# A fused attention and feed-forward kernel: first chunk in two token halves, first groups of 2, 2, 4 and 8 slices, all steps reordered

## The chip, the cores and the metric

The kernel runs on one core of a Trainium2 chip. The metric is the time on the device of that core, in microseconds (us). Most executions of one kernel lie within 1% of each other. An execution that is more than 1.5% above the fastest of its kernel is called slow.

## The reference

A sketched attention (four batches, four heads, 1088 tokens, 32 columns a head) is followed by a feed-forward with a rational activation:

```python
def phi(x):                                   # 8 x 8 features a token and head
    a = np.einsum('rd,bhsd->bhsr', S1, x)
    b = np.einsum('rd,bhsd->bhsr', S2, x)
    return np.einsum('bhsi,bhsj->bhsij', a, b).reshape(*x.shape[:-1], r * r)

q_p, k_p = phi(q), phi(k)
kv  = np.einsum('bhsf,bhsd->bhfd', k_p, v)    # one small matrix a batch and head
z   = np.sum(k_p, axis=2)
x   = np.einsum('bhsf,bhfd->bhsd', q_p, kv) / (np.einsum('bhsf,bhf->bhs', q_p, z)[..., None] + 1e-06)
# x becomes 4352 tokens x 128
h = x @ w_in                                  # 128 -> 2048
P = a[0] + a[1] * h + a[2] * h**2 + a[3] * h**3
Q = 1.0 + abs(b[0]) * abs(h) + abs(b[1]) * h**2
out = (P / (Q + 1e-06)) @ w_out               # 2048 -> 128
```

## The kernel before

The tokens run in chunks of 512 (the last is 256). The 2048 hidden columns are 16 slices of 128, and a group is a few slices of one chunk that share their operations. The program is a list of steps, each with an engine, the steps it needs and the buffers it takes and gives. Three tables written ahead of time decide the rest: `ORDER` (the sequence in which the steps are issued; it fixes each engine's queue), `ENGINE` (ScalarE or VectorE for a step that either can do) and `HOME` (which PSUM buffer a small result uses).

```python
FIRST = [4, 4, 8]      # slices in the groups of the first chunk
LAST = [8, 4, 4]       # slices in the groups of the last, short chunk; all others: 8, 8
# ... ENGINE, HOME, ORDER = [27, 4, 26, 30, ...]  (589 steps)

def issue(self, order):
    # ... each step in turn: its needs must be done, its buffers free
    for i in order:
        s = self.steps[i]
        s["fn"]()
```

A chunk's x is made in one piece: numerator and denominator (PE), division (VectorE), transposes (PE), copy to `xT` with a sign (either engine). Step names: `q0.nd0`, `q0.nd1`, `q0.dv`, `q0.xt`, `q0.xe`.

```python
def divide():
    nb = min(2, nt)
    nd = pair("nd")[:, :nt // nb, :nb * 132].rearrange("p b (g c) -> p b g c", c=D + 1)
    den = new("den", n)[:, :nt // nb, :nb * H]
    nc.vector.tensor_scalar(out=den, in0=nd[:, :, :, D], scalar1=1e-6, scalar2=None, op0=AX.add)
    nc.vector.reciprocal(out=den, in_=den)
    # ... x = nd * den
def x_transposes():
    p = new(*ps(nm, "xT"))
    for i in range(nt):
        nc.tensor.transpose(p[:, i * 128:(i + 1) * 128], in_=T["x", n][:, i, :], identity=ident)
```

A group g then goes through these steps; the letters are the step names used below:

```python
# h0, h2, ..: hidden matmuls, two slices each (PE), into h_ps
# e0, e2, ..: cast to bf16 hb (ScalarE, sometimes VectorE)
# ab: u = |hb|     sq: s = hb*hb      hi: t = a3*hb + a2
# cu: t = t*s      lo: hb = a1*hb+a0  (all VectorE)
def add(dst, src, name):                      # us: u += s  and  ts: t += hb
    d, s = T[dst, g][:, :gw], T[src, g][:, :gw]
    if ENGINE.get(name) == "DVE":
        nc.vector.tensor_add(out=d, in0=d, in1=s)
    else:
        nc.gpsimd.dma_start(out=d, in_=s, accum_op=AX.add, max_dma_last_dim=4096)
# ln: L = log(lsc*u + 1), ex: u = exp(-L)     (ScalarE)
# ov: t = t*u (VectorE)   pj: projection (PE)
```

So the first sum `us` and the second sum `ts` of nearly every group are accumulating transfers, and ScalarE's logarithm waits for the first.

## Time and profile before

| | before |
|---|---|
| median of 3 runs | 251.03 us (249.64 to 251.61) |
| span of the profiled execution | 248.8 us |
| accumulating transfers (first queue; 0.52 MB of it loads `w_out`) | 34.87 MB, 79.7% of the 16 engines' time |

The table by stretch is the view on which the explanation rests. Columns: stretch, length, then busy time and number of instructions of PE, PE's weight loads, VectorE (DVE), ScalarE (ACT) and GpSimd (POOL), then the granted clock, the DMA share and GB/s. The prediction shows its row for 20 to 30 us; these are further rows of the kernel before:

```profile
30.00:40.00 10.00, 9.86 (x59) 4.94 (x58) 9.90 (x12) 8.92 (x8) 1.72 (x2) 1.00 1.18 166
40.00:120.00 80.00, 78.38 (x682) 44.35 (x680) 74.98 (x59) 73.35 (x60) 15.67 (x12) 1.00 0.96 185
120.00:140.00 20.00, 19.99 (x186) 11.14 (x184) 19.90 (x15) 19.90 (x15) 3.57 (x3) 1.00 0.96 177
205.00:252.00 47.00, 24.86 (x215) 18.81 (x213) 37.73 (x35) 37.15 (x21) 8.36 (x8) 0.85 0.83 156
```

To read it: length less busy time is what an engine idled. VectorE idles 0.10 us between 120 and 140 us and 5.02 us between 40 and 120.

### The profile page before, as it was taken

How to read it: one execution, taken by the hardware profiler on the slowest of the kernel's cores; microseconds unless marked ns; L12 is line 12 of the kernel's file. 1: busy time of each engine (PE TensorE's matmuls, PEld its weight loads, DVE VectorE, ACT ScalarE, POOL GpSimd, SP SyncE). 2: the span in 40 equal slices, each digit the busy share in tenths (PEclk: the TensorE clock that was granted, in tenths of full speed). 3: DMA queues.
4: the chain of work that ended last, by engine and by line, in shares of the span. 5: the costliest groups of instructions: out<-in, count | busy, mean ns of one | idle time of the engine just before them, and what ended most of it. 6: DMA issues, size and time to landing. Idle time of an engine off the chain costs nothing.

```text
span 248.8 us, 4279 instructions
## 1 busy us (share of the span) xinstructions
PE 222.5 (89%) x1789; PEld 127.1 (51%) x1789; DVE 225.4 (91%) x205; ACT 213.7 (86%) x158; POOL 48.8 (20%) x61
## 2 busy tenths in 40 slices
PE   7999999999999999998999899999998969920763
PEld 2674455654636465553657354546453627720532
DVE  0785999998989989998999999999999999998993
ACT  3335589989989798989999999899999899899990
POOL 4000422132101212121111221122031312113210
PEclk9999999999999999999999999999999999995599
DMA  5994498999998899979999999999999999999982
GB/s 149 315 278 172 72 147 173 174 219 185 176 169 182 147 192 223 232 166 173 169 177 202 171 171 171 211 169 171 189 172 186 182 201 187 179 184 186 200 162 68
DMA packets 23427, 45.11 MB, mean 181 GB/s; under 512 B 5232, under 2 KB 13552, under 8 KB 23408
## 3 DMA queue, kind: packets, MB, share of 16 engines
q0 software_dynamic: 11232, 34.87, 79.7%
q1 hardware_dynamic: 11712, 9.90, 12.6%
q8 instruction: 14, 0.23, 0.4%
q10 hardware_dynamic: 464, 0.08, 0.2%
q14 instruction: 5, 0.04, 0.0%
HBM read 8.79 MB, written 2.23 MB: 44 GB/s over the span
## 4 chain that ended last, share of the span: by engine, by line
DVE 31%; PE 31%; DMA 20%; ACT 10%; issue 8%; SPq 0%; DVEq 0%; ACTq 0%; POOLq 0%
PE h_ps L572 15%; DMA u<-s 12%; DVE t L621 7%; DVE s L582 6%; DMA t<-hb 5%; DVE t L607 4%; DVE u L585 4%; PE h_ps L499 4%; ACT u L618 4%; DVE t L603 3%; PE out_ps L629 3%; ACT L L614 3%; DVE hb L610 2%; ACT hb L184 2%; DMA q<-in_q_dram 2%
## 5 line engine op out<-in xcount | busy, mean ns | idle before, releaser
L572 PE MATMUL h_ps<-xT,w_in_sb 128*128 128x512 f32 (+1 forms) x288 | 126.0, 577 | 4.2 <-ACT hb L184 2.7
L572 PEld LDWEIGHTS h_ps<-xT,w_in_sb 128*128 128x128 f32 x288 | 51.7, 190 | 56.5 <-issue 43.1
L184 ACT CAST hb<-h_ps 128x1024 bf16<-128x1024 f32 x66 | 64.8, 1020 | 8.2 <-PE h_ps L572 7.8
L614 ACT ACTIVATE L<-u,one_ap,lsc 128x4096 f32<-128x4096 bf16 (+2 forms) x20 | 65.9, 3295 | 6.4 <-DMA u<-s 6.3
L618 ACT ACTIVATE u<-L 128x4096 bf16<-128x4096 f32 (+2 forms) x20 | 62.3, 3116 | 0.2
L629 PE MATMUL out_ps<-w_out,t 128*128 128x128 bf16 x544 | 35.2, 225 | 15.8 <-DVE t L621 15.7
L594 POOL DMA_DIRECT2D u<-s x19 | 24.1, 1269 | 118.9 <-DVE u L585 54.5
L629 PEld LDWEIGHTS <-t 128*128 128x128 bf16 x544 | 32.5, 101 | 23.8 <-DVE t L621 20.6
L621 DVE TENSOR_TENSOR t<-t,u 128x4096 bf16<-128x4096 bf16 (+2 forms) x20 | 39.2, 1968 | 4.0 <-ACT u L618 2.2
L582 DVE TENSOR_TENSOR s<-hb 128x4096 bf16<-128x4096 bf16 (+2 forms) x20 | 39.2, 1963 | 1.5 <-ACT hb L184 1.5
L607 DVE TENSOR_TENSOR t<-t,s 128x4096 bf16<-128x4096 bf16 (+2 forms) x20 | 39.3, 1967 | 0.3
L594 POOL DMA_DIRECT2D t<-hb x18 | 21.6, 1200 | 72.2 <-issue 20.1
L610 DVE TENSOR_SCALAR hb<-hb,a_sb 128x4096 bf16<-128x4096 bf16 (+2 forms) x20 | 23.8, 1189 | 0.2
L603 DVE TENSOR_SCALAR t<-hb,a_sb 128x4096 bf16<-128x4096 bf16 (+2 forms) x20 | 23.6, 1183 | 0.0
L585 DVE TENSOR_SCALAR u<-hb 128x4096 int16<-128x4096 int16 (+2 forms) x20 | 22.3, 1115 | 0.1
L499 PE MATMUL h_ps<-qT,Srep 64*128 64x512 f32 (+1 forms) x72 | 19.5, 617 | 0.4 <-ACT hb L184 0.4
L506 DVE TENSOR_TENSOR q_pT<-A_sb,h_ps 128x1024 f32<-128x1024 f32 (+1 forms) x9 | 10.4, 1157 | 2.6 <-ACT A_sb L184 1.4
L519 PEld LDWEIGHTS h_ps<-kv,q_pT 128*64 128x64 f32 (+1 forms) x288 | 8.7, 134 | 5.1 <-issue 2.0
L519 PE MATMUL h_ps<-kv,q_pT 128*64 128x66 f32 (+1 forms) x288 | 10.1, 224 | 0.0
L184 ACT COPY A_sb<-h_ps 128x1024 f32<-128x1024 f32 (+1 forms) x9 | 8.7, 965 | 0.8 <-PE h_ps L499 0.8
L499 PEld LDWEIGHTS h_ps<-qT,Srep 64*128 64x128 f32 x72 | 5.4, 184 | 6.9 <-ACT hb L184 2.1
L184 ACT COPY kT<-h_ps 128x512 f32<-128x512 f32 x5 | 2.9, 585 | 5.3 <-PE h_ps L383 4.8
(89 smaller groups left out, 137.0 us busy)
## 6 DMA issues: line engine op xcount, KB each, us to landing
u<-s POOLq DMA_DIRECT2D x15, 1024.0 KB, 8.6
t<-hb POOLq DMA_DIRECT2D x15, 1024.0 KB, 9.5
k_sb<-in_k_dram SPq DMA_DIRECT2D x4, 512.0 KB, 4.3
q<-in_q_dram SPq DMA_DIRECT2D x8, 256.0 KB, 4.9
v<-in_v_dram SPq DMA_DIRECT2D x4, 512.0 KB, 8.2
out_dram<-oT SPq DMA_DIRECT2D x8, 256.0 KB, 7.0
w_in_sb<-in_moe_w_in_dram SPq DMA_DIRECT2D x2, 512.0 KB, 4.8
u<-s POOLq DMA_DIRECT2D x2, 512.0 KB, 7.7
```

The source lines that it names most:

```text
L184: nc.scalar.copy(out=out, in_=in_)
L499: nc.tensor.matmul(pair(i)[:, g, :W], lhsT=Srep[i][rows].rearrange("p g f -> p (g f)"), rhs=T["qT", n][rows, :W], start=True, stop=True)
L572: nc.tensor.matmul(p[:, i * W:(i + 1) * W], lhsT=w_in_sb[:, fi * 128:(fi + 1) * 128], rhs=T["xT", n][:, :W], start=True, stop=True)
L582: nc.vector.tensor_mul(out=new("s", g)[:, :gw], in0=h, in1=h)
L585: nc.vector.tensor_scalar(out=new("u", g)[:, :gw].bitcast(mybir.dt.int16), in0=T["hb", g][:, :gw].bitcast(mybir.dt.int16), scalar1=0x7FFF, ...
L594: nc.gpsimd.dma_start(out=d, in_=s, accum_op=AX.add, max_dma_last_dim=4096)
L603: nc.vector.tensor_scalar(out=new("t", g)[:, :gw], in0=T["hb", g][:, :gw], scalar1=a_sb[:, 3:4], scalar2=a_sb[:, 2:3], op0=AX.mult, op1=AX ...
L607: nc.vector.tensor_mul(out=T["t", g][:, :gw], in0=T["t", g][:, :gw], in1=T["s", g][:, :gw])
L614: nc.scalar.activation(out=new("L", g, l0)[:, :lw], in_=T["u", g][:, l0:l0 + lw], func=ACT.Ln, bias=one_ap, scale=lsc)
L618: nc.scalar.activation(out=T["u", g][:, l0:l0 + lw], in_=T["L", g, l0][:, :lw], func=ACT.Exp, scale=-1.0)
L621: nc.vector.tensor_mul(out=T["t", g][:, :gw], in0=T["t", g][:, :gw], in1=T["u", g][:, :gw])
L629: nc.tensor.matmul(T["out_ps", n][:, j * 128:(j + 1) * 128], lhsT=T["t", g][:, c:c + 128], rhs=W_out[:, fis[i], :], start=fis[i] == 0 and ...
```

## The change

Its intent: VectorE and ScalarE idle in the first 25 us, so the first chunk's x is made in two halves of 256 tokens, and its first feed-forward groups are small, so that VectorE starts on them earlier. Then every step was ordered anew, with other choices of engine and buffer. The core of the diff (the three tables are cut, and so is an unused variant that goes):

```diff
-FIRST = [4, 4, 8]
+FIRST = [2, 2, 4, 8]
+SPLIT = [0]
 # ENGINE, HOME and ORDER: all replaced (ORDER now has 604 steps)
-        def divide():
+        def divide(part=None):
             nb = min(2, nt)
-            nd = pair("nd")[:, :nt // nb, ...]
+            b0, b1 = (0, nt // nb) if part is None else (part, part + 1)
+            nd = pair("nd")[:, b0:b1, ...]
             ...
-        def x_transposes():
+        def x_transposes(part=None):        # the transposes of one half
-        def x_evac():
+        def x_evac(part=None):              # the copy of one half to xT
+        if n in SPLIT:
+            out = []
+            for i in range(2):
+                s = plan.add(f"{nm}.dv{i}", "DVE", 830, lambda i=i: divide(i), after=[nd[i]] + out[-1:], ...)
+                s = plan.add(f"{nm}.xt{i}", "PE", 240, lambda i=i: x_transposes(i), after=[s], ...)
+                out.append(add_copy(f"{nm}.xe{i}", lambda i=i: x_evac(i), W // 2, ...))
+            return out
...
+            if n in SPLIT and fis[s] == 0:   # first pair of slices: one half of the tokens at a time
+                hm = plan.add(f"{nm}.i{s}", "PE", 880, lambda s=s: h_mm(s, 0), ...)
+                hm = plan.add(f"{nm}.h{s}", "PE", 880, lambda s=s: h_mm(s, 1), ...)
```

## The prediction

> **What bounds the kernel now.** I read the page's busy shares first, then the forty slices, then the table by stretch, then the gaps of VectorE in order of time, and the chain of waits last.
>
> ```profile
> PE 222.5 (89%) x1789; PEld 127.1 (51%) x1789; DVE 225.4 (91%) x205; ACT 213.7 (86%) x158; POOL 48.8 (20%) x61
> ...
> DVE  0785999998989989998999999999999999998993
> ACT  3335589989989798989999999899999899899990
> ...
> DMA  5994498999998899979999999999999999999982
> ```
>
> The averages name VectorE (91%), with PE, ScalarE and the DMA engines close behind. The slices (6.2 us each) show where the missing 9% lies: VectorE is at 0, 7, 8 and 5 tenths in the first four and near full from 25 us on. In slices 4 and 5 (19 to 31 us) the DMA engines are at 4 tenths and ScalarE at 5.
>
> ```profile
> 20.00:30.00 10.00, 10.00 (x27) 4.69 (x28) 8.37 (x13) 5.04 (x7) 2.56 (x2) 1.00 0.29 79
> 40.00:60.00 20.00, 19.51 (x201) 11.37 (x200) 18.64 (x16) 18.26 (x17) 4.95 (x4) 1.00 0.96 185
> 140.00:160.00 20.00, 19.15 (x143) 10.29 (x142) 19.82 (x17) 18.98 (x12) 3.78 (x3) 1.00 1.01 186
> 220.00:235.00 15.00, 3.41 (x33) 3.41 (x34) 13.72 (x13) 14.90 (x7) 3.83 (x4) 0.59 1.04 189
> ```
>
> The columns are stretch, length, busy time of PE, PEld, DVE, ACT and POOL, granted clock, DMA share and GB/s. From 40 us on nothing is free: of 20 us, VectorE works 18.6 to 19.8, ScalarE 18.3 to 19.0, and the DMA share is 0.96 to 1.01. Only 20 to 30 us has room: there PE computes the first hidden slices and the others wait for them. In 220 to 235 PE is nearly done, while ScalarE and DMA are full.
>
> ```profile
> 16.73 0.69 DVE L529 TENSOR_TENSOR x<-h_ps,den 128x512 f32<-128x512 f32 x1
> 17.34 1.21 DVE L403 TENSOR_TENSOR k_p<-a_t,w_ps 128x1024 f32<-128x1024 f32 x1
> 19.95 1.22 DVE L506 TENSOR_TENSOR q_pT<-A_sb,h_ps 128x1024 f32<-128x1024 f32 x1 [1.41 <-ACT A_sb L184]
> ...
> 24.68 1.23 DVE L582 TENSOR_TENSOR s<-hb 128x2048 bf16<-128x2048 bf16 x1 [1.46 <-ACT hb L184]
> ```
>
> VectorE divides the first chunk's x at 16.2 to 17.4 us, but squares its first hidden group only at 24.68, after gaps of 1.41 and 1.46 us. Between them lie four transposes, the copy of x to xT (18.33, 0.69 us), the first hidden matmuls (from 19.90) and two casts (21.92 and 23.63), since a group of 4 slices needs two casts. This stretch is what the change attacks. Later gaps are small and have several owners:
>
> ```profile
> 59.88 2.29 DVE L621 TENSOR_TENSOR t<-t,u 128x4096 bf16<-128x4096 bf16 x1 [0.74 <-ACT u L618]
> 71.22 1.22 DVE L506 TENSOR_TENSOR q_pT<-A_sb,h_ps 128x1024 f32<-128x1024 f32 x1 [0.67 <-PE h_ps L499]
> ...
> 90.59 0.29 DVE L186 COPY a_t<-w_ps 128x128 f32<-128x128 f32 x1 [0.99 <-PE w_ps L392]
> ```
>
> The seven larger ones between 41 and 116 us are 0.49, 0.74, 0.67, 0.40, 0.99, 0.68 and 0.65: 4.6 us in all. From 120 to 222 us VectorE is busy 100.57 of 102.
>
> ```profile
> DVE 31%; PE 31%; DMA 20%; ACT 10%; issue 8%; SPq 0%; DVEq 0%; ACTq 0%; POOLq 0%
> ```
>
> The chain of waits moves from engine to engine: no single wait can be removed for its full length.
>
> **What the Trainium skill says.** "Perfetto Trace Analysis", section "Optimizing Scalar/DVE Operations": if these engines are not saturated but cause bubbles on others, "breaking up instructions may allow work to be completed sooner". That is the idea here, and the trace agrees that both have room before 25 us and not after. "VectorE: DVE Perf Modes", section "The TRN2 errata": a large tile pays a fixed cost once, many small tiles pay it each. The trace agrees: the bf16 product takes 2288, 1215 and 686 ns for 4096, 2048 and 1024 columns, so 0.524 ns a column and some 140 ns fixed. "DMA: Bandwidth & Descriptors", section "Issuing engines are not separate DMA queues": all transfers share 16 engines and interleave. The trace agrees: an accumulate of 256 KB landed in 3.7 us at the quiet end, and two others of that size took 7.4 in the median.
>
> **The change part by part.** I decoded both orders into the sequence of steps on each engine; the number of fill matmuls stays (15 of 16 run), and no arithmetic changes. The unused path with four weight copies goes: no instruction of it ran.
>
> *The start.* Up to the key-value products of the first batch (PE until 13.6) the queues are nearly the same. Then, with durations of the trace: the two kv copies end at 14.6 (one on each engine, as before); the first half's numerator matmuls take 0.55 (half of 1.09), to 15.4; an expansion of the second chunk (1.06) follows, then the other half's 0.55, to 17.0. The first half's division (0.16+0.20+0.43, as in the last chunk's rows of half the width) runs beside them, to 16.3. Its two transposes end at 17.3, its copy to xT, now on VectorE (0.48), at 17.9; the second division at 18.7. PE meanwhile does a key projection (0.6) and the second expansion (1.06), so the second transposes end at 19.2 and their copy at 19.7. The first half's hidden matmuls stand in PE's queue behind those transposes, so the two halves gain little by themselves: 19.2 to 20.1 for both slices. The cast of a group of two slices is one (20.2 to 21.2, before: the second ended at 24.64). VectorE, which first does the small constants (1.05) and a key product (1.13), begins the first group at 22.0 in place of 24.68. Its gaps in this stretch are then some 0.5 and 0.6 us in place of 1.41 and 1.46, with work enough after 22 because slices 4 to 7 arrive next and slices 2 and 3 are left for later: **1.7 us saved**.
>
> *What VectorE pays.* Two divisions for one: 2 x (159+203+425) - (170+253+691) = +0.46 us. The copy to xT moves from ScalarE: 2 x 477 ns = +0.95. One more group (2048 columns become two of 1024): six operations more; by their starts (1.13 becomes 2 x 0.60 for a product, 0.72 becomes 2 x 0.46 for a scalar operation) about +0.67. The other moves between the engines nearly cancel: 9.95 us leave VectorE (one 2048-column sum of each kind at 1.22, one of 1024 at 0.69, two casts, three output copies, four smaller) and 9.22 come (three sums of 1024 columns, three casts, two output copies, six smaller): -0.73. Sum: **+1.35 us**.
>
> *ScalarE*: -0.69 for the copy, +0.4 for one more pair of logarithm and exponential (2 x 1242 - 2097 and 2 x 1057 - 1913, less overlap), -0.3 for the rest: **-0.6 us**, no relief worth counting.
>
> *DMA.* The sums done by accumulate were 67,584 + 66,560 columns and become 68,608 + 67,584, because VectorE takes three small ones in place of two of 2048 and one of 1024: +1.5%. Their queue took 79.7% of 248.8 us, so 198 us: **+3.0 us** of transfer. Against it the first sum is issued at about 23.3 in place of 26.83, and the engines were idle from 22 to 28.
>
> *Sum.* On VectorE -1.7 + 1.35 = -0.35 us. The larger hope is the middle: the first sums land some 3 us earlier, so logarithms fill ScalarE while PE still makes hidden slices, and PE finishes seven of the first chunk's eight pairs of slices about 1.5 us earlier. I assume that two fifths of the 4.6 us of gaps go, 1.85 us; this is a choice, not a reading. That makes -2.2 us: 251.0 - 2.2 = **248.8 us**.
>
> **Rivals.** *The gain is eaten.* ScalarE sets the pace to the end: from 217.76 it runs to 243.1 almost without a gap. From its first cast at 21.92 it idles 15.7 us; it starts 1.5 us earlier in the change, but 1.9 us of small work done before that point has moved away or later. If its later gaps stay, nothing is won: 251. Its waits for first sums speak for this rival (6.3 us in eight waits, second only to those for hidden matmuls, 7.8), since the DMA work grows. *DMA becomes the bound.* With 3.0 us more transfer and a start 3.5 us earlier, a full DMA would end at the same time: 250.5 to 252. Against: VectorE waited only 1.8 us for the second sums in the whole run. *The new order dissolves the middle gaps.* All 4.6 us gone with -0.35 gives 246.1; for it speaks that each such gap is under 1 us and that an order can be searched for; against it that PE, ScalarE and DMA are over 95% busy there. *A worse tail.* The last groups need the same ScalarE work in the same order of sizes, about 25 us, and the last product and store cost the same; I count nothing either way.
>
> **Range and chances.** From full failure with one new wait (251.8) to nearly all gaps gone (245.8): that should hold 8 times in 10. Faster by over 2% needs 246.0 or less, thus every gap: 0.12. Slower by over 2% would need 5 us of new waits: 0.04. Within 2%: 0.84.
>
> **What would show it.** Right: the first group's operation on VectorE at about 22 us in place of 24.68; VectorE's busy time 226 to 227.5, its idle time down by 3 to 4 us from 23.4; the DMA share in 20 to 30 us well over 0.29; fewer gaps of VectorE from 41 to 116 us. Wrong: busy time up and idle time the same, or longer waits of ScalarE for the first sums (over 6.3 us), or a gap at the halves' copies over 2 us, would mean that the gain was eaten. A first group at 24 us or later would mean that the halves wait behind PE's other work more than I count. A time under 246 would mean that the order, not the halves, was the change's main part.

## The result, and the profile after

The changed kernel gives the reference's result. It took 253.38 us in the median of 4 runs (252.96 to 253.9), the kernel before 250.82 in 4 runs beside it. Ratios here and below are the mean time of one kernel's fast runs over that of the other's of the same rounds, so they are not quite the ratios of the medians: this one is 1.0107, with a 95% interval of 1.0062 to 1.0152. A second measurement of five rounds on another chip (below) gave 1.0082. The change makes the kernel about 1% slower, and the predicted range (up to 251.8) did not hold it.

The busy line and the slices of the changed kernel:

```profile
PE 223.7 (89%) x1788; PEld 129.0 (51%) x1793; DVE 225.8 (90%) x218; ACT 213.2 (85%) x157; POOL 50.6 (20%) x63
...
DVE  0878989979999999899997999989999999999793
ACT  2423869789999979899889999988999999898991
...
DMA  5890998998999999989999889999999999999972
```

VectorE's work grew by 0.4 us only, but its span grew by 2.6: its idle time rose from 23.4 to 25.6 us. New sevens and eights stand in the middle of its row, where before there were nines. How VectorE's start went (start, duration, engine, line, operation, tiles; in brackets the idle time before it and its cause):

```profile
17.75 0.48 DVE L539 TENSOR_SCALAR xT<-h_ps,sig 128x256 f32<-128x256 f32 x1 [0.48 <-PE h_ps L528]
...
19.79 0.48 DVE L539 TENSOR_SCALAR xT<-h_ps,sig 128x256 f32<-128x256 f32 x1 [0.79 <-PE h_ps L528]
...
22.57 0.43 DVE L593 TENSOR_SCALAR u<-hb 128x1024 int16<-128x1024 int16 x1 [0.25 <-ACT hb L187]
```

The start came as intended: both halves' copies at 17.75 and 19.79 us, and the first group's operation at 22.57 us in place of 24.68. The table by stretch, for the changed kernel:

```profile
20.00:30.00 10.00, 10.00 (x45) 5.30 (x45) 9.57 (x17) 5.92 (x7) 3.38 (x3) 1.00 0.55 63
30.00:40.00 10.00, 10.00 (x73) 5.42 (x72) 8.91 (x13) 8.10 (x10) 1.26 (x2) 1.00 1.07 226
40.00:120.00 80.00, 77.11 (x643) 43.89 (x644) 75.68 (x62) 73.61 (x60) 16.87 (x14) 1.00 0.96 185
120.00:140.00 20.00, 19.42 (x210) 11.72 (x209) 17.91 (x14) 18.46 (x15) 3.73 (x3) 1.00 0.96 177
205.00:252.00 47.00, 26.81 (x218) 19.20 (x218) 39.36 (x37) 38.80 (x22) 8.55 (x8) 0.92 0.87 166
```

VectorE's idle time by stretch, worked out as length less busy time from such rows (the last stretch ends with the span; 0 to 20 and 140 to 205 us are from rows not shown):

| stretch (us) | before | changed |
|---|---|---|
| 0–20 | 9.22 | 9.05 |
| 20–30 | 1.63 | 0.43 |
| 30–40 | 0.10 | 1.09 |
| 40–120 | 5.02 | 4.32 |
| 120–140 | 0.10 | 2.09 |
| 140–205 | 1.25 | 1.57 |
| 205–end | 6.07 | 7.04 |

Three things are to be seen. The 1.20 us won from 20 to 30 us are given back by 40 us, all but 0.2. The gaps from 40 to 120 us shrink by 0.7 us. And from 120 us on the new order opens 3.3 us of new gaps, 2.3 of them before 205 us, where the kernel before had hardly any. The chain of waits of the changed kernel:

```profile
PE 44%; DVE 22%; ACT 17%; DMA 11%; issue 5%; ACTq 0%; DVEq 0%
```

PE has 44% of the chain, where it had 31%: the end is now followed back more often to a hidden matmul that came late. ScalarE's waits say the same (engine, line, waited for: us in total, times, longest), first of the kernel before, then of the changed one:

```profile
ACT hb L184 <- PE h_ps L572: 7.8, 12, 1.6
ACT L L614 <- DMA u<-s: 6.3, 8, 1.2
```

```profile
ACT hb L187 <- PE h_ps L580: 14.1, 19, 2.9
...
ACT L L622 <- DMA u<-s: 3.7, 3, 1.5
```

The waits for the first sums fell by 2.6 us, as an earlier start should make them, but the waits of the casts for hidden matmuls rose by 6.3, half of it (4.2 to 7.3) in the first 40 us and half (3.7 to 6.8) from 40 to 205.

### The profile page after: what moved, and what is told of

Its sections match the earlier page's. It is cut to its first block, busy times and chain, and to the rows that moved or that the text cites.

```text
span 251.4 us, 4292 instructions
## 1 busy us (share of the span) xinstructions
PE 223.7 (89%) x1788; PEld 129.0 (51%) x1793; DVE 225.8 (90%) x218; ACT 213.2 (85%) x157; POOL 50.6 (20%) x63
## 3 DMA queue, kind: packets, MB, share of 16 engines
q0 software_dynamic: 11520, 35.39, 79.8%
## 4 chain that ended last, share of the span: by engine, by line
PE 44%; DVE 22%; ACT 17%; DMA 11%; issue 5%; ACTq 0%; DVEq 0%
PE h_ps L580 26%; ACT L L622 9%; DMA u<-s 8%; DVE s L590 5%; PE h_ps L483 5%; DVE t L629 5%; ACT u L626 5%; DVE t L615 4%; PE out_ps L637 3%; DVE t L611 3%; PE h_ps L503 2%; ACT hb L187 2%; DVE u L593 2%; DMA q<-in_q_dram 2%; DMA k_sb<-in_k_dram 2%
## 5 line engine op out<-in xcount | busy, mean ns | idle before, releaser
L602 POOL DMA_DIRECT2D t<-hb x19 | 22.5, 1185 | 88.7 <-issue 21.8
L618 DVE TENSOR_SCALAR hb<-hb,a_sb 128x4096 bf16<-128x4096 bf16 (+2 forms) x21 | 24.5, 1168 | 0.2
L593 DVE TENSOR_SCALAR u<-hb 128x4096 int16<-128x4096 int16 (+2 forms) x21 | 21.5, 1023 | 2.6 <-ACT hb L187 2.4
L483 PE MATMUL h_ps<-qT,Srep 64*128 64x512 f32 (+1 forms) x72 | 18.9, 612 | 1.1 <-ACT xT L537 0.6
L387 DVE TENSOR_TENSOR k_p<-a_t,w_ps 128x1024 f32<-128x1024 f32 x6 | 7.3, 1214 | 0.0
```

The costliest lines, as they stand in the source:

```text
L483: nc.tensor.matmul(pair(i)[:, g, :W], lhsT=Srep[i][rows].rearrange("p g f -> p (g f)"), rhs=T["qT", n][rows, :W], start=True, stop=True)
L593: nc.vector.tensor_scalar(out=new("u", g)[:, :gw].bitcast(mybir.dt.int16), in0=T["hb", g][:, :gw].bitcast(mybir.dt.int16), scalar1=0x7FFF, ...
```

## The experiments

The theory after the two traces: (A) PE, which idles 0.14 us from 20 to 50 us in the kernel before, sets the pace, so an earlier start of VectorE only puts off work that PE must do later, and the loss comes from single waits of the new order after 80 us. The rivals: (B) the halves or the small groups themselves cost the time; (C) the larger amount of accumulating transfers (35.39 MB for 34.87) makes DMA the bound; (D) the new tail alone is to blame. The texts before the runs name their theories by letters of their own. All 18 kernels run gave correct results and were timed in five rounds; the medians of the kernel before beside them were 250.66 to 251.09 us. "Slower" here says that the interval lies above 1; over 2% slower is only new_start_old_rest, and new_to_165_then_old is unclear.

### The parts of the change, alone or taken away

**after_no_halves**: the changed kernel with the first chunk's x in one piece.

```diff
-SPLIT = [0]
+SPLIT = []
 # ORDER: q0.dv1 -> q0.dv, q0.xt1 -> q0.xt, q0.xe1 -> q0.xe; dv0, xt0, xe0 and g0.i0 left out
```

> The changed kernel with the first chunk's x made in one piece again (its division, transposes and copy stand where the second half's stood; groups 2, 2, 4, 8 and all other order kept). Theory A (the new order behind the first chunk makes the loss, the start is neutral): 253.4 us +- 0.6, since the halves only let two quarter matmuls go 0.4 us earlier. Theory B (the start itself makes the loss: more and smaller operations, work put off): 0.5 to 1.0 us faster than the changed kernel, since two divisions and two copies become one each.

Measured: 254.63 us, 1.0154 [1.0123, 1.0186]. It is slower than the changed kernel by some 0.5%, and in its trace everything is late by 0.6 to 0.7 us from the first hidden matmul to the end. Neither theory had it: one said 253.4 +- 0.6, the other less than the changed kernel. Inside the new order the halves help a little.

**before_with_halves**: the old order, with each of the first chunk's steps replaced by its two halves.

```diff
+SPLIT = [0]
 # ORDER: ... q0.nd0, q0.dv0, ... q0.nd1, q0.dv1, q0.xt0, q0.xt1, q0.xe0, q0.xe1, ... g0.i0, g0.h0
```

> The kernel before with the halves alone (groups 4, 4, 8, copies on ScalarE as before, order otherwise kept; the first hidden matmuls still stand behind the same key projection on PE). Theory A: 250.8 us +- 0.6, nothing won or lost. Theory B: 251.3 to 251.8, the added operations cost.

Measured: 254.5 us, 1.0134 [1.0094, 1.0174], slower, and above what either theory had said. The line of its trace that explains it, PE's second half of numerators:

```profile
16.92 0.69 PE L486 MATMUL h_ps<-kv,q_pT 128*64 128x66 f32 x16 [1.23 <-DVE x L500]
```

PE stood 1.23 us until VectorE had read the first half's numerators, because nothing was put between the two; the first hidden matmul came 1.8 us later, and the end 2.5. In the changed order another expansion of 1.13 us stands there. This run tells of a bad place in the queue, not of what halves cost.

**before_with_groups**: the old order, x in one piece, groups of 2, 2, 4 and 8.

```diff
-FIRST = [4, 4, 8]
+FIRST = [2, 2, 4, 8]
 # ORDER: g0's steps become those of two groups at the same places
```

> The kernel before with its first feed-forward groups cut as in the change (2, 2, 4, 8), x in one piece and all else in the old order. It pays six more VectorE operations (about 0.7 us) and some 1.5% more accumulate work, and its first sum goes out earlier. My theory (VectorE's early start buys nothing as PE leads): 250.9 to 252.5. The rival, that the groups are what makes the new start better: 249.5 to 250.5.

Measured: 251.23 us, 1.0008 [0.9971, 1.0045], the same. (My text was wrong in one thing: the transfers did not grow; they are 34.87 MB as before.) VectorE idled 0.18 us from 20 to 30 us (before: 1.63), 1.72 from 30 to 40 (before: 0.10) and 0.5 less than before from 40 to 205. This is the change's local gain in its purest form, and it is paid back within 10 us. No step of PE was moved here: VectorE, ahead of PE, waits 0.77 us at 32.04 for the second chunk's numerators and 0.65 us at 37.88 for a cast.

**before_pe_delayed**: the kernel before, with eight useless matmuls ahead of the first hidden ones on PE.

```diff
-            for _ in range(2):
+            for _ in range(8 if i == 3 else 2):      # one fill of 8, issued before k11.pr
                 nc.tensor.matmul(p[:, :CW], lhsT=zeros...
```

> The kernel before, with eight idle fill matmuls (1.72 us of PE time, nothing reads them) put ahead of the first chunk's hidden matmuls. Theory C (from the first hidden matmul on the whole run hangs on one chain through PE and ScalarE, and a shift at the start is carried to the end in full): +1.7 us, 252.5. Rival (VectorE's 23 us of gaps or the later waits absorb it): +0.5 us or less.

Measured: 253.67 us, 1.011 [1.008, 1.0141], so 2.7 us more. PE's hidden matmuls begin at 21.89 in place of 19.90, 2.0 us later:

```profile
21.89 6.28 PE L563 MATMUL h_ps<-xT,w_in_sb 128*128 128x512 f32 x14
```

What is put ahead of these matmuls on PE is paid in full at the end (2.0 to 3.5 us by the interval). VectorE, which waits for the same matmuls, is put off with PE: it idles 12.85 us up to 40 us in place of 10.96, and from 40 to 205 us 6.80 for 6.38. So the run shows that its gaps do not absorb a delay at this place; which of the two engines sets the pace after it, the run does not tell.

### Where in the run the loss lies

Two pairs of kernels take one order up to a cut and the other after it, with their choices of engine and buffer. At a cut, the steps that one order has done and the other not must be fitted in by hand, which is a seam that can cost time.

```diff
-ORDER = <new order>
+ORDER = <new order up to the cut> + <all other steps in the old order>      # and the reverse
```

**new_start_old_rest** and **old_start_new_rest** cut at about 35 us.

> The changed kernel's order up to the copy of the second chunk's x (about 35 us: halves, groups 2, 2, 4, 8), then the order and the engine choices of the kernel before for all that is left; the hidden slices 2 and 3 and the second key projection, which the start put off, come first. Theory A: 250.0 to 251.2 us, the loss is gone. Theory B: 252.5 to 253.5, the loss stays.

> The order of the kernel before up to the same copy (about 35 us, groups 4, 4, 8, no halves), then the changed kernel's order and engine choices for all that is left. Theory A: 252.7 to 254 us, as slow as the changed kernel. Theory B: 250.5 to 251.3, as fast as before.

Measured: 257.54 us, 1.0254 [1.0203, 1.0304], and 255.4 us, 1.0169 [1.014, 1.0197]. Both are slower than either kernel, as no theory had it. VectorE was busy only 13.41 and 14.06 of the 20 us from 40 to 60, where the two kernels have 18.64 and 18.15: the seams cost some 4 us and more. (The profile of the first was of a slow execution, and that of the second of its longest, 257.69 us; they are used for nothing finer.) Inconclusive.

**new_to_80_then_old** and **old_to_80_then_new** cut at 80 us, where the traces of the two kernels are nearly level.

> The changed kernel's order and engine choices up to about 80 us (halves, groups 2, 2, 4, 8 and the put-off work all done there), then those of the kernel before; the seam was chosen where the two kernels differ by three steps. Theory D (the new start is neutral, PE has caught up by 80 us, and the loss is made in single waits of the new order after that): 250.5 to 251.5. Rival E (the start's extra work is what costs): 252.5 to 253.5.

> The mirror image: the kernel before up to about 80 us (no halves, groups 4, 4, 8), then the changed kernel's order and engine choices. Theory D: 252.7 to 254. Rival E: 250.5 to 251.5.

Measured: 250.72 us, 1.0014 [0.9972, 1.0055], and 254.06 us, 1.0132 [1.0089, 1.0176]. This pair decides. With the old order after 80 us the kernel is as fast as before, whichever start it has; with the new order after 80 us it is as slow as the changed one, whichever start. Rivals B and C fall with it: both hybrids move 35.13 MB by accumulating transfers, and they are 3.3 us apart. (They issue 14 and 16 of the fills, pairs of useless matmuls, where the two kernels issue 15; what that is worth was not tried.) Two rows of the fast hybrid, then the same of the slow one:

```profile
120.00:140.00 20.00, 19.80 (x183) 10.90 (x181) 19.90 (x15) 19.90 (x15) 3.77 (x4) 1.00 1.00 184
...
205.00:252.00 47.00, 23.72 (x206) 18.24 (x206) 36.92 (x35) 36.38 (x20) 8.36 (x8) 0.84 0.81 152
```

```profile
120.00:140.00 20.00, 19.55 (x210) 11.69 (x209) 18.01 (x14) 18.57 (x15) 3.73 (x3) 1.00 0.96 179
205.00:252.00 47.00, 29.04 (x218) 21.22 (x218) 39.46 (x37) 38.77 (x22) 8.88 (x8) 0.85 0.87 165
```

In the fast one the idle 2 us of VectorE between 120 and 140 are gone again (19.90 of 20). In the slow one they are there, behind the old start, with the same wait for a cast at 134.02 us (1.35 us; in the changed kernel 1.68). A seam at 80 us is not what makes it slow: from 80 to 120 us VectorE idles 2.03 us in it, 1.98 in the changed kernel.

**new_to_165_then_old** and **old_to_165_then_new** were to halve the rest.

> The changed kernel up to about 170 us, then the kernel before. By the shifts of the two traces there (ScalarE 2 to 3 us behind, VectorE 1 us) Theory D with the loss made between 80 and 170 us gives 252.5 to 253.5; if most of it is made in the last 80 us, 250.8 to 251.8.

> The kernel before up to about 165 us, then the changed kernel. Loss made between 80 and 170 us: 250.7 to 251.7; made in the last 80 us: 252.3 to 253.5.

Measured: 256.35 us, 1.0208 [1.0165, 1.0252], and 254.04 us, 1.0126 [1.0097, 1.0155]. The seam shows again: from 165 to 175 us PE is busy 6.82 of 10 in the first and ScalarE 6.30 of 10 in the second. They cannot place the loss.

**old_to_205_then_new** gives the old kernel the new tail.

> The old order up to the step where about 205 us have passed, then the new order of the tail. By the comparison of work done, the new order's loss is complete by 175 us, so the tail is neutral: with a clean seam 250.7 to 251.7 (ratio 1.000 to 1.004). The rival, that the new tail (its chain of waits ends in ScalarE's logarithms and two waits of about 1 us for the first sums) costs what is lost: 253 to 254.

Measured: 252.87 us, 1.0072 [1.0034, 1.0111]. It is level with before at 205 us (VectorE's busy time up to there 187.87 and 187.67, ScalarE's 176.77 and 176.59) and ends 1.8 us later. A part of this is the seam (ScalarE waits 1.95 us for a hidden matmul at 208.83); the other part is a wait that every kernel with the new tail has. ScalarE's large logarithms in the tail that waited for a first sum: the one of the kernel before, then the two of the changed kernel, then the one of this hybrid:

```profile
217.76 3.80 ACT L614 ACTIVATE L<-u,one_ap,lsc 128x4096 f32<-128x4096 bf16 x1 [0.70 <-DMA u<-s]
```

```profile
219.19 3.81 ACT L622 ACTIVATE L<-u,one_ap,lsc 128x4096 f32<-128x4096 bf16 x1 [0.99 <-DMA u<-s]
...
229.52 3.80 ACT L622 ACTIVATE L<-u,one_ap,lsc 128x4096 f32<-128x4096 bf16 x1 [1.21 <-DMA u<-s]
```

```profile
228.94 3.80 ACT L605 ACTIVATE L<-u,one_ap,lsc 128x4096 f32<-128x4096 bf16 x1 [1.81 <-DMA u<-s]
```

Before, ScalarE waits once for a first sum in the tail, 0.70 us, and runs on almost without a gap; in the new tail it waits 1.8 to 2.2. From 205 us on the accumulating transfers have 6.82 MB to move in the changed kernel, 6.55 before, because in the new tail VectorE makes a first sum of 1024 columns itself and before it made one of 2048. That the extra 0.27 MB causes the wait is argued, and one run speaks against it: two_waits_mended (below) moves 6.55 MB from 205 us on and still waits 1.9 us there. Nor is a longer idle time in the tail the new tail's alone: before_with_groups, with the old one, idles 7.02 us from 205 us on.

### Mending single waits of the new order

In the changed kernel's traces these waits stood out after 80 us. ScalarE waits for a first sum and only then makes three small copies, so PE waits too; and VectorE waits for a cast, because 80 key-value products stand in PE's queue before the hidden matmuls:

```profile
92.02 3.81 ACT L622 ACTIVATE L<-u,one_ap,lsc 128x4096 f32<-128x4096 bf16 x1 [1.54 <-DMA u<-s]
...
96.48 0.65 PE L471 MATMUL w_ps<-ident,q 128*128 128x128 f32 x4 [1.64 <-ACT kT L187]
```

```profile
127.42 2.08 PE L405 MATMUL w_ps<-v,k_p 128*64 128x64 f32 x64
...
130.04 3.70 PE L580 MATMUL h_ps<-xT,w_in_sb 128*128 128x512 f32 x8
...
134.02 1.23 DVE L593 TENSOR_SCALAR u<-hb 128x4096 int16<-128x4096 int16 x1 [1.68 <-ACT hb L187]
```

**kv_after_hidden** puts these products behind the next hidden matmuls; **copies_before_log** puts the copies ahead of the logarithm; **three_waits_mended** does both, and issues a first sum of the tail earlier.

```diff
-g10.h6, k30.kv, k31.kv, k3.rem, ..., g9.hi, q5.dv, g9.cu, q6.A, g10.h4, g10.e4
+g10.h6, g9.hi, q5.dv, g10.h4, g9.cu, q6.A, g10.e4, g10.e6, k30.kv, k31.kv, k3.rem, ...     # kv_after_hidden
-g6.ln0, k31.tr, g5.pj, k31.ev, q3.xt, q3.xe, q5.tr, q5.ev
+k31.tr, k31.ev, q3.xt, q3.xe, q5.tr, q5.ev, g5.pj, g6.ln0                                  # copies_before_log
-g16.ts, ..., g17.us
+g17.us, g16.ts                                                                             # the tail
```

> The changed kernel with the last batch's 80 key-value matmuls (2.6 us of PE) put behind the hidden matmuls of slices 4 and 5 of the group that VectorE waits for at 134.02 us (gap 1.68). Theory C with the loss in single waits of the new order: 1.3 to 1.7 us faster than the changed kernel, 251.7 to 252.1. Rival (the loss is spread over everything, each gap closed opens elsewhere): within 0.4 us of it.

> The changed kernel with ScalarE's three small copies at 95.8 to 97.4 us put ahead of the logarithm that waited for its DMA (92.02), and the 1.8 us projection on PE put behind the transposes that those copies wait for, so that PE need not wait 1.64 us at 96.48. Theory C: 1.0 to 1.9 us faster than the changed kernel. Rival: within 0.4 us of it.

> Both of these edits, and in the tail the absolute value of the last large group ahead of its first scalar operation and its sum issued ahead of the sum of the group before (the logarithm waited 1.21 us for it at 229.52). Theory C: 3 to 4 us faster than the changed kernel, 249.5 to 250.5, as fast as before or faster. Rival: 252.5 or more.

Measured: 252.57 us, 1.007 [1.0027, 1.0113]; 252.36 us, 1.0055 [1.0032, 1.0078]; 254.8 us, 1.0154 [1.013, 1.0177]. The wait at 134 us goes in the first:

```profile
132.74 1.23 DVE L576 TENSOR_SCALAR u<-hb 128x4096 int16<-128x4096 int16 x1 [0.20 <-ACT hb L170]
```

VectorE's idle time from 120 to 140 us falls by 1.3 us (2.09 to 0.76), but 0.5 of it comes back from 140 to 205 us (1.57 to 2.10) and 0.3 in the tail. The third kernel was a miss: by moving one sum ahead of another it made VectorE wait 3.9 us for the one put back:

```profile
230.62 2.29 DVE L612 TENSOR_TENSOR t<-t,u 128x4096 bf16<-128x4096 bf16 x1 [3.94 <-DMA t<-hb]
```

**two_waits_mended** leaves that third edit out, and **after_again** measures the changed kernel once more.

> The changed kernel with the two mends that each won about 1 us alone (the key-value products behind the hidden matmuls at 130 us, and the three small copies ahead of the logarithms at 92 us), without the third, the tail's, that cost. If the two waits are separate losses, they add up: 253.4 - 0.9 - 1.3 = 251.2. If what one gives is taken back by the next wait, as the traces of the three together hinted up to 178 us, it is no better than the better one alone: 252.2 to 252.6.

> The changed kernel as it is, five rounds on one chip, since its first result has only four executions and the mended ones are measured against it. Theory: the ratio stays near 1.011 (1.008 to 1.014), so that each mended wait gives 0.4 to 0.5% of it back. Rival: its first ratio was high by chance, near 1.006, and the mends gave nothing.

Measured: 252.04 us, 1.0045 [1.0006, 1.0085], and 253.52 us, 1.0082 [1.0051, 1.0113]. By the middle values the two mends together give back about 0.4 to 0.6% of the 0.8 to 1.1% lost, hardly more than the better one alone (1.0055). The intervals overlap, also with that of the changed kernel measured again (1.0051 to 1.0113), so that the mends shorten the run is likely and not shown. In the trace of the two mends VectorE idles 2.3 us less from 40 to 140 us than in the changed kernel (6.41 to 4.16), but 0.5 more from 140 to 205 (2.03) and 0.2 more in the tail (7.27): a part of what is mended in the middle is waited for again later. The second profile of the changed kernel has the same gap from 120 to 140 us (1.84 us) and a smaller tail (6.29): the tail's idle time differs from execution to execution, the middle's hardly. So how much of the mend arrives depends on the profile that it is held against: the span is 1.2 us shorter than in the first and 0.4 us shorter than in the second.

### The start with the old order behind it

Since the new start did no harm with the old order after it, its parts were tried there: **new_to_80_no_halves** (x in one piece) and **new_to_80_q1_first** (the second chunk's load issued before the third's, since PE waits for it at the start).

```diff
-SPLIT = [0]                                   # new_to_80_no_halves
+SPLIT = []
-ORDER = [..., ld.q2, ..., ld.q1, ...]         # new_to_80_q1_first
+ORDER = [..., ld.q1, ld.q2, ...]
```

> The same kernel of 250.7 with the first chunk's x made in one piece again. In the full changed kernel the halves were worth 0.6 to 1.2 us, all of it carried to the end. If that holds with the old order behind it: 251.3 to 251.9. If the old order absorbs it: 250.7.

> The kernel with the new order to 80 us and the old one after it (250.7), with the first load of the second query chunk issued ahead of the third's. In the start PE waited some 0.4 us for that load. If a shift at the start is carried to the end, as the two kernels with fills or whole chunks suggest, it ends at 250.3; if DMA or ScalarE absorb it, at 250.7.

Measured: 251.01 us, 1.0007 [0.9966, 1.0048], and 251.89 us, 1.0036 [0.9996, 1.0075]. Neither wins; the load order, if anything, loses. No kernel beats the kernel before: the best three, new_to_80_no_halves, before_with_groups and new_to_80_then_old (1.0007 to 1.0014), are equal to it within their intervals of 0.4%.

## Why the prediction was wrong, point by point

VectorE's account, in us, of the profiled executions (248.8 and 251.4):

| term | predicted | measured | second profile |
|---|---|---|---|
| idle at the start (0–40) | −1.7 | −0.38 | −0.25 |
| work of VectorE | +1.35 | +0.4 | +0.6 |
| gaps of the middle (40–205) | −1.85 | +1.61 | +1.21 |
| tail (205–end) | 0 | +0.97 | +0.22 |
| sum | −2.2 | +2.6 | +1.8 |

**Right.** The first group's operation at 22.57 us (predicted 22.0), its first sum issued at 23.91 (predicted 23.3), the two copies to xT ending at 18.2 and 20.3 (17.9 and 19.7), the halves' hidden matmuls standing in PE's queue (from 19.59; predicted 19.2), the DMA share of 20 to 30 us at 0.55, ScalarE's work (213.7 to 213.2; predicted −0.6). ScalarE's waits for first sums fell, as the hope of earlier sums had it.

**Off in size.** The start: 1.20 us were saved from 20 to 30 us, near enough to what was worked out, but 0.99 were lost again from 30 to 40. The prediction counted "work enough after 22" for VectorE and did not follow PE past that point: PE had been busy 10.00 of 10 us from 20 to 30, as the prediction's own table showed, and the slices and the second key projection that were put off (1.72 and 0.62 us by the durations of the trace) had to be done from 30 to 40. VectorE, ahead of PE, waited there: 0.52 us for the second chunk's numerators and 0.36 for a cast. The groups alone show the same, 1.45 us won and 1.62 lost, though there PE puts nothing off. So the clause "PE finishes seven of the first chunk's eight pairs of slices about 1.5 us earlier" was borne out (2.6 us by the casts below) and is no gain: it left out the work put off behind them, and so the premise of the hope failed with it. The casts of the seventh and the eighth pair in the changed kernel, then of the last pair in the kernel before:

```profile
33.89 1.01 ACT L187 CAST hb<-h_ps 128x1024 bf16<-128x1024 f32 x1 [1.38 <-PE h_ps L580]
...
36.49 1.01 ACT L187 CAST hb<-h_ps 128x1024 bf16<-128x1024 f32 x1 [0.52 <-PE h_ps L580]
```

```profile
36.45 1.01 ACT L184 CAST hb<-h_ps 128x1024 bf16<-128x1024 f32 x1 [0.28 <-PE h_ps L572]
```

All eight are ready no sooner, and PE begins the second chunk's hidden matmuls at 39.80 us in place of 36.69. VectorE's own work was over-counted by 0.95. About half of that is the extra group: before_with_groups has its six added operations and 225.6 us of work, 0.2 more than before, where the prediction had 0.67. The rest I did not take apart.

Two readings of the prediction were wrong beside this. ScalarE is not "over 95% busy" where the middle gaps lie (73.35 of the 80 us from 40 to 120, 92%). And from its first cast to 243.1 us it idles 15.1 us by the view of stretches, not 15.7.

**The step that failed.** "I assume that two fifths of the 4.6 us of gaps go, 1.85 us; this is a choice, not a reading." The gaps from 40 to 120 us did shrink, by 0.70 us. But the step treated a change of all 589 steps as something that could only close gaps. In the stretches where the kernel before had next to none (0.10 us from 120 to 140, 1.25 from 140 to 205) a new order could only open some, and it opened 2.3 us there. This term is off by 3.5 us, of a whole miss of 4.8 (+2.6 for −2.2). The exchange of orders at 80 us shows that it is the order after 80 us, with its choices of engine and buffer, and not the new start, that costs: 1.0014 against 1.0132.

**The tail.** "I count nothing either way" was wrong by 0.2 to 1.0 us: ScalarE waits twice for first sums there.

**The rivals.** "The gain is eaten" named the start's fate, but its 251 assumed that nothing new would be lost. "DMA becomes the bound" is not borne out: with the same bytes the two hybrids differ by 3.3 us. The range ended at full failure "with one new wait (251.8)"; there were several.

**What stays open.** By the middle values the two mended waits account for about half of the loss; the noise allows much less and much more. The rest lies after 80 us. Whether the tail's waits for first sums are a part of it, or even most of it (rival D), cannot be said: the one mend tried there made another wait, and the cuts at 165 and 205 us have seams of their own. Nor was the new sequence after 80 us tried apart from the new choices of engine and buffer there.

## What to carry to other kernels

Before hoping for an earlier start on one engine, look in the same stretch for the engine without a gap (here PE, 10.00 of 10 us) and ask what work on it is put off: an engine that starts earlier on part of the input waits later for the rest. A wholesale new order is a part of the change of its own and can lose what the idea behind it wins; exchange the orders at a point where the two traces are level, and run both halves, before judging the idea. A stretch that has no gaps left has only gaps to gain, so a range must leave room on that side.

## What the Trainium skill lacked or had wrong

- "Perfetto Trace Analysis", section "Optimizing Scalar/DVE Operations": "breaking up instructions may allow work to be completed sooner" is said of Scalar and Vector operations that cause bubbles on other engines. Here the bubbles were VectorE's own, PE was full, and I applied the sentence all the same. VectorE then started 2.1 us sooner, and nothing was completed sooner: 1.0008 for the groups alone, 1.0014 for the new start with the old order behind it. The page does not say that the broken-up rest must still pass through the full engine.
- The same page, section "Identifying the Most-Contended Engine", says that the engine of the highest occupancy is the most contended and to be optimized first; for the tensor engine, the share of peak arithmetic and the weight-load time are to be read in place of matmul busy time. Here VectorE had the highest (91%) and weight loads only 51% (the share of peak was not worked out). Yet an operation group on VectorE that started 1.55 us earlier (before_with_groups, 23.13 in place of 24.68 us) left the time at 1.0008. In a kernel with four engines at 86% or more, the averages did not tell where an earlier start pays.
- "DMA: Bandwidth & Descriptors", section "Issuing engines are not separate DMA queues", gives no time for an accumulating transfer, and I found none on its other parts. In the changed kernel such a transfer of 1 MB landed 9.2 us after its issue in the median, a first sum of 256 KB 3.5 us; in the kernel before, two first sums of 256 KB took 7.4.
